# An attention-plus-MLP kernel on one core: x taken transposed out of the values product, head pairs placed on row and column tiles, the MLP spread by hand

## The chip, the cores and the metric

The kernel runs on one core of a Trainium2 chip. The metric is device time in microseconds (us), the median of the runs shown. The core's engines work beside each other: TensorE (PE, and PEld for the loading of its weights), VectorE (DVE), ScalarE (ACT), GpSimd (POOL) and SyncE (SP, here only a queue of DMAs).

## The reference

Eight batches of attention with 12 heads, 448 tokens and 64 values per head, whose softmax has one more term in its denominator, feed an MLP with a squared ReLU.

```python
# q, k, v: (8, 12, 448, 64) f32; w_in: (768, 2048); w_out: (2048, 768)
scores = (1 / sqrt(64)) * q @ k.T                 # 448 x 448 per head
m = max(scores); e = exp(scores - m)
attn = e / (sum(e) + exp(-m) + 1e-9)              # = exp(s) / (sum(exp(s)) + 1)
x = (attn @ v), heads side by side                # 3584 x 768
out = square(maximum(x @ w_in, 0)) @ w_out        # 3584 x 768 f32
```

## The kernel before

`load_batch` (L79) brings one batch of q, k and v in as fp16 with tokens in the partitions: four chunks of 112 tokens, twelve DMAs on POOL's queue (L84 to L86), each moving 112 x 12 runs of 64 values, which are 256 bytes of the f32 source. `load_weights` follows on the same queue (L94, L96). Two batches and the weights are issued before anything else; batch b + 2 is issued after batch b's attention.

`attn_pair` (L98) does two heads. PE transposes the pair's q and k (8 small matmuls, L104 and L109, into the PSUM tile `tp`), DVE copies them to `qkt` (L117 to L119); k lies there twice, once with the upper and once with the lower 64 partitions set to zero by two POOL memsets (L115, L116), so that a product over all 128 partitions gives one head's scores. Per head four matmuls of 448 columns give the scores, keys in the partitions (L130, PSUM `stp`), ACT takes the exponential of two of them at a time (L137, to `et`), and 16 matmuls of 65 columns (L147, PSUM `op`) multiply a 112 x 112 block of `et`, which is loaded as the weights, with the values and a column of ones. So the output has query tokens in its partitions and the sum of exponentials in column 64. DVE adds 1, inverts and multiplies (L157, L164, L165, to `xc`). The MLP needs x with features in the partitions: SP writes `xc` to DRAM (L173) and reads it back with a transposing DMA to `xt` (L177).

The MLP is cut into seven blocks of 512 tokens. `mm1_unit` (L186) does 128 of the 2048 hidden features: six matmuls of 512 columns (L190, PSUM `mp`), then ReLU and squaring on DVE (L198, L204). `mm2_unit` (L207) does 128 tokens by 512 or 256 outputs: 16 matmuls (L213), a scaled copy on ACT (L225), and a DMA out on ACT's queue. One block is 16 + 8 units; after each pair `drain_moe(4)` puts four units into the order of the work, from batch 2 on, block b - 2 being queued with batch b. A scheduler of the framework may reorder instructions of an engine from this program order. The last block comes after all attention.

Of the kernel before, what the change touches and what calls it, by code (L numbers as in the profile page):

```python
# [8 lines left out]
FP32 = mybir.dt.float32  # L10
FP16 = mybir.dt.float16
BF16 = mybir.dt.bfloat16
# [5 lines left out]
def kernel(  # L18
# [14 lines left out]

    P = 112
    NC = S // P
# [3 lines left out]
    TBLK = 512  # L39
    NTB = NT // TBLK  # L40
    NSUB = TBLK // 128

# [6 lines left out]
    qkv_pool = ctx.enter_context(tc.tile_pool(name="qkv", bufs=2))  # L49
    qkt_pool = ctx.enter_context(tc.tile_pool(name="qkt", bufs=4))  # L50
    et_pool = ctx.enter_context(tc.tile_pool(name="et", bufs=4))
    xc_pool = ctx.enter_context(tc.tile_pool(name="xc", bufs=3))
    small = ctx.enter_context(tc.tile_pool(name="small", bufs=8))
    g_pool = ctx.enter_context(tc.tile_pool(name="g", bufs=1))
    r_pool = ctx.enter_context(tc.tile_pool(name="r", bufs=3))
    osb_pool = ctx.enter_context(tc.tile_pool(name="osb", bufs=2))

    st_psum = ctx.enter_context(tc.tile_pool(name="st_psum", bufs=2, space=bass.MemoryType.PSUM))
    o_psum = ctx.enter_context(tc.tile_pool(name="o_psum", bufs=1, space=bass.MemoryType.PSUM))
    tp_psum = ctx.enter_context(tc.tile_pool(name="tp_psum", bufs=1, space=bass.MemoryType.PSUM))  # L60
    moe_psum = ctx.enter_context(tc.tile_pool(name="moe_psum", bufs=2, space=bass.MemoryType.PSUM))

    ident = consts.tile([128, 128], FP16)
    make_identity(nc, ident)

    xt_tiles = [persist.tile([128, NT], FP16, name=f"xt_{c}") for c in range(DCH)]
    win_tiles = [persist.tile([128, DF], FP16, name=f"win_{c}") for c in range(DCH)]
    wout_tiles = [persist.tile([128, DM], FP16, name=f"wout_{c}") for c in range(NFFB)]

    xs_dram = [nc.dram_tensor(f"xstage_{b}", (NPAIR, S, 128), FP16, kind="Internal").ap()  # L70
               for b in range(B)]

    q_r = q.rearrange("b h (c p) d -> b c p h d", p=P)
    k_r = k.rearrange("b h (c p) d -> b c p h d", p=P)
    v_r = v.rearrange("b h (c p) d -> b c p h d", p=P)

    qkv_tiles = {}

    def load_batch(b):  # L79
        qb = qkv_pool.tile([P, NC, H, D], FP16, name="qb")  # L80
        kb = qkv_pool.tile([P, NC, H, D], FP16, name="kb")
        vb = qkv_pool.tile([P, NC, H, D + 1], FP16, name="vb")
        for c in range(NC):
            nc.gpsimd.dma_start(out=qb[:, c, :, :], in_=q_r[b, c])  # L84
            nc.gpsimd.dma_start(out=kb[:, c, :, :], in_=k_r[b, c])  # L85
            nc.gpsimd.dma_start(out=vb[:, c, :, :D], in_=v_r[b, c])  # L86
        nc.gpsimd.memset(vb[:, :, :, D], 1.0)
        qkv_tiles[b] = (qb, kb, vb)

    def load_weights():  # L90
        win_r = moe_w_in.rearrange("(c p) f -> c p f", p=128)
        wout_r = moe_w_out.rearrange("(c p) f -> c p f", p=128)
        for c in range(DCH):
            nc.gpsimd.dma_start(out=win_tiles[c][:, :], in_=win_r[c])  # L94
        for c in range(NFFB):
            nc.gpsimd.dma_start(out=wout_tiles[c][:, :], in_=wout_r[c])  # L96

    def attn_pair(b, pr):  # L98
        hA = 2 * pr
        qb, kb, vb = qkv_tiles[b]  # L100

        qkt_ps = tp_psum.tile([128, 2, S], FP16, name="tp")
        for c in range(NC):
            nc.tensor.transpose(  # L104
                qkt_ps[:, 0, c * P:(c + 1) * P],
                qb[:P, c, hA:hA + 2, :],
# [185 lines left out]
```

## Time and profile before

| What | Value |
|---|---|
| time, median of 2 runs (587.69 and 588.19) | 587.94 us |
| span of the profiled execution | 585.7 us |
| PE busy in the span | 494.6 us (84%) |
| PE weight loads busy | 301.5 us |
| DVE busy | 236.1 us (40%) |
| ACT busy | 197.8 us (34%) |
| POOL busy | 148.7 us (25%) |
| mean granted PE clock | 0.976 |
| HBM read and written | 45.61 MB and 16.52 MB |

The span runs from the first to the last instruction of one profiled execution. That execution has no time of its own in the records, so its span stands beside the median of the runs, which is 2.2 us longer. Busy PE time counts overlapping matmuls once, and the ends of matmuls are modelled. In the rows of groups the columns are: line, engine, operation, tile written and tiles read, shapes, count, then busy time, the mean ns of one, and the engine's idle time just before them with what ended it.

### The profile page before, as it was taken

The page shows a single profiled execution, that of the slowest core. Times are in us where ns is not written, and L with a number is a line of the kernel's source. Part 1 is how long each engine was busy: PE and PEld are TensorE (multiplying, and loading weights), DVE is VectorE, ACT ScalarE, POOL GpSimd, SP SyncE. Part 2 cuts the span into 40 slices and gives each one's busy share as a digit, 9 for nine tenths or more (in the row PEclk, how much of TensorE's full clock was granted, in tenths as well). Part 3 has the DMA queues.
Part 4 walks back from the last instruction along what each step waited for, and adds up shares of the span by engine and source line. Part 5 has one row for each costly group of instructions (what it writes and reads, how often), then busy time and mean ns, then how long its engine had stood idle before and what let it go on. Part 6 is the DMA issues. An engine that isn't in the chain of part 4 may idle for free.

```text
span 585.7 us, 9469 instructions
## 1 busy us (share of the span) xinstructions
PE 494.6 (84%) x3872; PEld 301.5 (51%) x3872; DVE 236.1 (40%) x656; ACT 197.8 (34%) x249; POOL 148.7 (25%) x228
## 2 busy tenths in 40 slices
PE   0100998497999899997999889997999999999997
PEld 0000766364566455564656555564555665566454
DVE  0100555155641276315661157511674237721830
ACT  0000677262433224332434323432325334333011
POOL 9644555531015301071102601134101000000000
PEclk9999999698999899999999989999899999999999
DMA  9999599949119911299113940179111221022002
GB/s 108 128 194 208 96 131 99 123 60 61 32 25 127 148 25 24 60 135 113 25 27 83 162 60 17 32 106 167 25 25 25 71 71 32 20 62 71 21 28 81
DMA packets 183114, 45.44 MB, mean 78 GB/s; under 512 B 176672, under 2 KB 178720, under 8 KB 183072
## 3 DMA queue, kind: packets, MB, share of 16 engines
q0 software_dynamic: 133728, 22.81, 53.3%
q1 hardware_dynamic: 45312, 11.02, 10.5%
q10 hardware_dynamic: 4032, 11.01, 5.1%
q8 instruction: 30, 0.49, 0.3%
q14 instruction: 12, 0.10, 0.1%
HBM read 45.61 MB, written 16.52 MB: 106 GB/s over the span
## 4 chain that ended last, share of the span: by engine, by line
PE 72%; DMA 18%; POOL 4%; issue 2%; DVE 2%; ACT 1%; SPq 0%; POOLq 0%; DVEq 0%
PE mp L190 25%; PE mp L213 20%; PE op L147 14%; PE stp L130 11%; DMA xt<-xstage 6%; DMA xstage<-xc 4%; DMA vb<-in_v_dram 3%; DMA win<-in_moe_w_in_dram 2%; DMA kb<-in_k_dram 1%; POOL vb L86 1%; POOL qb L84 1%; DMA wout<-in_moe_w_out_dram 1%; PE tp L104 1%; PE tp L109 1%; ACT et L137 1%
## 5 line engine op out<-in xcount | busy, mean ns | idle before, releaser
L137 ACT ACTIVATE et<-stp 112x896 f16<-112x896 f32 x192 | 169.1, 915 | 266.8 <-PE stp L130 265.9
L190 PE MATMUL mp<-xt,win 128*128 128x512 f16 x672 | 169.3, 386 | 26.0 <-DMA xt<-xstage 23.0
L213 PE MATMUL mp<-wout,g 128*128 128x512 f16 (+1 forms) x896 | 157.4, 326 | 0.0
L130 PE MATMUL stp<-qkt 128*112 128x448 f16 x384 | 101.5, 373 | 39.1 <-POOL qkt L115 38.3
L147 PEld LDWEIGHTS <-et 112*112 112x112 f16 x1536 | 101.4, 134 | 52.4 <-ACT et L137 27.5
L147 PE MATMUL op<-vb,et 112*112 112x65 f16 x1536 | 109.8, 219 | 4.5 <-DVE xc L165 2.2
L213 PEld LDWEIGHTS <-g 128*128 128x128 f16 x896 | 86.1, 98 | 50.0
L190 PEld LDWEIGHTS <-win 128*128 128x128 f16 x672 | 64.1, 100 | 90.3 <-issue 21.2
L198 DVE TENSOR_SCALAR rt<-mp 128x512 f16<-128x512 f32 x112 | 77.1, 689 | 56.6 <-PE mp L190 52.2
L115 POOL MEMSET qkt<- 64x448 f16 x48 | 22.4, 466 | 229.0 <-PE stp L130 122.4
L117 DVE COPY qkt<-tp 128x448 f16<-128x448 f16 x48 | 18.6, 387 | 137.1 <-PE tp L109 135.8
L130 PEld LDWEIGHTS <-qkt 128*112 128x112 f16 x384 | 41.3, 135 | 59.4 <-POOL qkt L115 38.5
L225 ACT ACTIVATE ot<-mp 128x512 f32<-128x512 f32 (+1 forms) x56 | 27.4, 490 | 116.8 <-PE mp L213 116.8
L157 DVE TENSOR_SCALAR zp<-op 112x4 f32<-112x4 f32 x96 | 15.5, 162 | 124.2 <-PE op L147 124.0
L204 DVE TENSOR_TENSOR g<-rt 128x512 f16<-128x512 f16 x112 | 47.2, 422 | 2.0
L165 DVE TENSOR_TENSOR xc<-op,rcp 112x256 f16<-112x256 f32 x96 | 40.6, 422 | 2.5
L84 POOL DMA_DIRECT2D qb<-in_q_dram x32 | 30.1, 940 | 37.3 <-PE tp L109 35.0
L104 PE MATMUL tp<-ident,qb 112*128 112x112 f16 x192 | 27.8, 220 | 12.6 <-DMA qb<-in_q_dram 11.1
L109 PE MATMUL tp<-ident,kb 112*128 112x112 f16 x192 | 27.5, 219 | 5.0 <-DMA kb<-in_k_dram 5.0
L86 POOL DMA_DIRECT2D vb<-in_v_dram x32 | 29.8, 935 | 7.4 <-PE mp L213 4.9
L85 POOL DMA_DIRECT2D kb<-in_k_dram x32 | 29.9, 935 | 0.0
L104 PEld LDWEIGHTS <-qb 112*128 112x128 f16 x192 | 19.3, 102 | 18.2 <-DMA qb<-in_q_dram 11.6
(15 smaller groups left out, 111.9 us busy)
## 6 DMA issues: line engine op xcount, KB each, us to landing
out_dram<-ot ACTq DMA_DIRECT2D x28, 384.0 KB, 2.6
qb<-in_q_dram POOLq DMA_DIRECT2D x32, 168.0 KB, 5.9
kb<-in_k_dram POOLq DMA_DIRECT2D x32, 168.0 KB, 6.1
vb<-in_v_dram POOLq DMA_DIRECT2D x32, 168.0 KB, 7.2
xstage<-xc SPq DMA_DIRECT2D x48, 112.0 KB, 2.0
win<-in_moe_w_in_dram POOLq DMA_DIRECT2D x6, 512.0 KB, 9.2
wout<-in_moe_w_out_dram POOLq DMA_DIRECT2D x16, 192.0 KB, 7.3
xt<-xstage SPq DMA_TRANSPOSE x48, 2.5
```

The lines of the kernel that those rows point to most:

```text
L84: nc.gpsimd.dma_start(out=qb[:, c, :, :], in_=q_r[b, c])
L86: nc.gpsimd.dma_start(out=vb[:, c, :, :D], in_=v_r[b, c])
L104: nc.tensor.transpose(qkt_ps[:, 0, c * P:(c + 1) * P], qb[:P, c, hA:hA + 2, :], ident[:P, :P],)
L109: nc.tensor.transpose(qkt_ps[:, 1, c * P:(c + 1) * P], kb[:P, c, hA:hA + 2, :], ident[:P, :P],)
L130: nc.tensor.matmul(stp[:P, jj, :S], qkt[:, 1 + hh, jc * P:(jc + 1) * P], qkt[:, 0, :], start=True, stop=True,)
L137: nc.scalar.activation(out=et[:P, 2 * half:2 * half + 2, :], in_=stp[:P, :, :S], func=AF.Exp, scale=scale,)
L147: nc.tensor.matmul(op[:P, ib, :], et[:P, jc, ib * P:(ib + 1) * P], vb[:P, jc, hA + hh, :], start=(jc == 0), stop=(jc == NC - 1),)
L165: nc.vector.tensor_tensor(out=xc[:P, :, h0:h0 + 64], in0=op[:P, :, :D], in1=rcp[:P, :].to_broadcast([P, NC, D]), op=ALU.mult,)
L190: nc.tensor.matmul(hp[:, :TBLK], win_tiles[dc][:, fb * 128:(fb + 1) * 128], xt_tiles[dc][:, t0:t0 + TBLK], start=(dc == 0), stop=(dc == DC ...
L198: nc.vector.tensor_scalar(out=rt[:, :], in0=hp[:, :TBLK], scalar1=0.0, scalar2=GS, op0=ALU.max, op1=ALU.mult,)
L204: nc.vector.tensor_mul(gt[:, :], rt[:, :], rt[:, :])
L213: nc.tensor.matmul(o2[:, :n1 - n0], gtiles[(t, fb)][:, ts * 128:(ts + 1) * 128], wout_tiles[fb][:, n0:n1], start=(fb == 0), stop=(fb == NF ...
```

## The change

- **Tokens.** A batch's 448 tokens lie as 64 partitions x 7 tokens (`RUN`): four of the seven in partitions 0 to 63, three in partitions 64 to 127. A run of a load is then four or three tokens, 1 KB or 768 bytes of the f32 source. Each cut of a batch takes eight DMAs; batch 0 comes in three cuts, the later ones whole, and the weights come in parts between and behind batches 0 and 1. `regroup` has DVE reorder q and k so that a transpose finds two heads side by side.
- **Scores.** No zeroed copies of k and no POOL memsets: head h uses partitions 64h to 64h + 63 of `qkt` as they are, so the two matmuls of a pair of heads address the two row halves of the array. Keys come as three groups of 128 and one of 64; for the last one head h also writes partitions 64h to 64h + 63.
- **Values.** The values are now the weights and `et` is the moving operand, 448 columns at a time. Head h writes partitions 64h to 64h + 63 of `xp`, so the two heads address the two column halves of the array. The output has features in the partitions: it is x transposed. A second set of matmuls with a matrix of 1/256 as weights writes the sum of exponentials to `zp`, repeated over the 64 partitions of each head.
- **Normalising.** ACT takes ln(zp + 1/256) and then exp of its negative; DVE multiplies `xp` by that straight into `xt`. The write to DRAM and the transposing DMA are gone. The factor 256 of the ReLU (L198) moves into this division.
- **MLP.** Blocks of 384 and 512 tokens in turn (3584 in all), the units cut into single matmuls by a generator. The order of the program is kept (`manual_schedule`). One pass of the main loop does the transposes of pair i + 1, half the scores of pair i, MLP work, the other half, the values of pair i - 1, MLP work, and the normalising of pair i - 1. A batch's block is spread over the six passes that follow its last pair, so the first seven passes have no MLP work. The transposes' PSUM tile `tp` now shares the two buffers `mp` of the MLP. Outputs go out on SP's queue, two DMAs for 128 tokens.

```diff
-    P = 112
-    NC = S // P
...
-    TBLK = 512
...
+    RUN = S // 64
+    LO = 4
+    HI = RUN - LO
...
+    nat = ctx.enter_context(tc.tile_pool(name="nat", bufs=2))
+    flat = ctx.enter_context(tc.tile_pool(name="flat", bufs=2))
+    qkt_pool = ctx.enter_context(tc.tile_pool(name="qkt", bufs=3))
+    e_pool = ctx.enter_context(tc.tile_pool(name="e", bufs=2))
+    z_pool = ctx.enter_context(tc.tile_pool(name="z", bufs=2))
+    g_pool = ctx.enter_context(tc.tile_pool(name="g", bufs=2))
+    osb_pool = ctx.enter_context(tc.tile_pool(name="osb", bufs=3))
+    s_psum = ctx.enter_context(tc.tile_pool(name="s_psum", bufs=2, space=bass.MemoryType.PSUM))
+    xz_psum = ctx.enter_context(tc.tile_pool(name="xz_psum", bufs=1, space=bass.MemoryType.PSUM))
+    m_psum = ctx.enter_context(tc.tile_pool(name="m_psum", bufs=2, space=bass.MemoryType.PSUM))
...
+    ctx.enter_context(tc.manual_schedule())
+    nc.scalar.preload_act_table_set("natural_log_exp_and_others")
+    ones = consts.tile([128, 64], FP16)
+    nc.vector.memset(ones, 1.0 / GS)
+    one_b = consts.tile([128, 1], FP32)
+    nc.vector.memset(one_b, 1.0 / GS)
+    xt = persist.tile([128, DCH, NT], FP16, name="xt")
+    win = persist.tile([128, DCH, DF], FP16, name="win")
+    wout = persist.tile([128, NFFB, DM], FP16, name="wout")
+    q_r = q.rearrange("b h (p t) d -> b p h t d", t=RUN)
+    k_r = k.rearrange("b h (p t) d -> b p h t d", t=RUN)
+    v_r = v.rearrange("b (g two) (p t) d -> b two p g t d", two=2, t=RUN)
+    win_r = moe_w_in.rearrange("(c p) f -> p c f", p=128)
+    wout_r = moe_w_out.rearrange("(c p) f -> p c f", p=128)
+    nats, flats = {}, {}
+    def load_batch(b, cuts):
+        qn = nat.tile([128, H, LO, D], FP16, name="qn")
+        kn = nat.tile([128, H, LO, D], FP16, name="kn")
+        vn = nat.tile([128, NPAIR, 2, LO, D], FP16, name="vn")
+        for p0, p1 in cuts:
+            hs = slice(2 * p0, 2 * p1)
+            for t, r in ((qn, q_r), (kn, k_r)):
+                nc.gpsimd.dma_start(out=t[0:64, hs, :, :], in_=r[b, :, hs, 0:LO, :])
+                nc.gpsimd.dma_start(out=t[64:128, hs, 0:HI, :], in_=r[b, :, hs, LO:RUN, :])
+            ps = slice(p0, p1)
+            nc.gpsimd.dma_start(out=vn[0:64, ps, 0, :, :], in_=v_r[b, 0, :, ps, 0:LO, :])
+            nc.gpsimd.dma_start(out=vn[64:128, ps, 0, 0:HI, :], in_=v_r[b, 0, :, ps, LO:RUN, :])
+            nc.gpsimd.dma_start(out=vn[0:64, ps, 1, 1:LO, :], in_=v_r[b, 1, :, ps, 0:HI, :])
+            nc.gpsimd.dma_start(out=vn[64:128, ps, 1, :, :], in_=v_r[b, 1, :, ps, HI:RUN, :])
+        nats[b] = (qn, kn, vn)
+    def load_win(i, n):
+        w = DF // n
+        nc.gpsimd.dma_start(out=win[:, :, i * w:(i + 1) * w], in_=win_r[:, :, i * w:(i + 1) * w])
+    def load_wout(i, n):
+        w = NFFB // n
+        nc.gpsimd.dma_start(out=wout[:, i * w:(i + 1) * w, :], in_=wout_r[:, i * w:(i + 1) * w, :])
+    def regroup(b, p0, p1):
+        hs = slice(2 * p0, 2 * p1)
+        n = 2 * (p1 - p0)
+        both = []
+        for t in nats[b][0:2]:
+            f = flat.tile([128, LO, H // 2, D], FP16, name=f"flat{len(both)}")
+            nc.vector.tensor_copy(f[:, 0:HI, 0:n, :], t[:, hs, 0:HI, :].rearrange("p h t d -> p t h d"))
+            nc.vector.tensor_copy(f[0:64, HI, 0:n, :], t[0:64, hs, HI, :])
+            both.append(f)
+        for pr in range(p0, p1):
+            flats[b, pr] = both, 2 * (pr - p0)
+    def transposes(b, pr):
+        both, h0 = flats.pop((b, pr))
+        hs = slice(h0, h0 + 2)
+        tp = m_psum.tile([128, 2, 512], FP16, name="mp")
+        for i, t in enumerate(both):
+            for s in range(LO):
+                np_ = 128 if s < HI else 64
+                nc.tensor.transpose(tp[:, i, 128 * s:128 * s + np_], t[0:np_, s, hs, :], ident[0:np_, 0:np_])
+        qkt = qkt_pool.tile([128, 2, S], FP16, name="qkt")
+        nc.vector.tensor_copy(qkt, tp[:, :, 0:S])
+        return qkt
+    def scores(qkt, et, ks):
+        for kk in ks:
+            if kk < HI:
+                sp = s_psum.tile([128, 2, 512], FP32, name="sp")
+                for h in range(2):
+                    r = slice(64 * h, 64 * h + 64)
+                    nc.tensor.matmul(sp[:, h, 0:S], qkt[r, 1, 128 * kk:128 * kk + 128], qkt[r, 0, :],
+                                     start=True, stop=True)
+                nc.scalar.activation(out=et[:, 2 * kk:2 * kk + 2, :], in_=sp[:, :, 0:S], func=AF.Exp, scale=scale)
+            else:
+                sp = s_psum.tile([128, 2, 512], FP32, name="sp")
+                for h in range(2):
+                    r = slice(64 * h, 64 * h + 64)
+                    nc.tensor.matmul(sp[r, 0, 0:S], qkt[r, 1, 128 * kk:S], qkt[r, 0, :],
+                                     start=True, stop=True)
+                nc.scalar.activation(out=et[:, 2 * kk, :], in_=sp[:, 0, 0:S], func=AF.Exp, scale=scale)
+    def values(b, pr, et):
+        vn = nats[b][2]
+        xp = xz_psum.tile([128, 512], FP32, name="xp")
+        zp = xz_psum.tile([128, 512], FP32, name="zp")
+        for kk in range(HI):
+            for dst, v in ((xp, True), (zp, False)):
+                for h in range(2):
+                    nc.tensor.matmul(dst[64 * h:64 * h + 64, 0:S],
+                                     vn[:, pr, h, kk + h, :] if v else ones[:, :],
+                                     et[:, 2 * kk + h, :], start=(kk == 0), stop=False)
+        for dst, v in ((xp, True), (zp, False)):
+            for h in range(2):
+                r = slice(64 * h, 64 * h + 64)
+                nc.tensor.matmul(dst[r, 0:S], vn[r, pr, h, HI * (1 - h), :] if v else ones[r, :],
+                                 et[r, 2 * HI, :], start=False, stop=True)
+        lnz = z_pool.tile([128, S], FP32, name="lnz")
+        rcp = z_pool.tile([128, S], FP32, name="rcp")
+        nc.scalar.activation(out=lnz, in_=zp[:, 0:S], func=AF.Ln, bias=one_b)
+        nc.scalar.activation(out=rcp, in_=lnz, func=AF.Exp, scale=-1.0)
+        return xp, rcp
+    def normalise(b, pr, xp, rcp):
+        nc.vector.tensor_mul(xt[:, pr, b * S:(b + 1) * S], xp[:, 0:S], rcp)
+    def mlp(t0, n):
+        gt = []
+        for fb in range(NFFB):
+            hp = m_psum.tile([128, 512], FP32, name="mp")
+            for dc in range(DCH):
+                nc.tensor.matmul(hp[:, 0:n], win[:, dc, fb * 128:(fb + 1) * 128], xt[:, dc, t0:t0 + n],
+                                 start=(dc == 0), stop=(dc == DCH - 1))
+                if dc < DCH - 1:
+                    yield n / 2.4
+            rt = r_pool.tile([128, 512], FP16, name="rt")
+            nc.vector.tensor_scalar(out=rt[:, 0:n], in0=hp[:, 0:n], scalar1=0.0, scalar2=None, op0=ALU.max)
+            g = g_pool.tile([128, 512], FP16, name=f"g{fb}")
+            nc.vector.tensor_mul(g[:, 0:n], rt[:, 0:n], rt[:, 0:n])
+            gt.append(g)
+            yield n / 2.4
+        for ts in range(n // 128):
+            ot = osb_pool.tile([128, DM], FP32, name="ot")
+            for n0, n1 in ((0, 512), (512, DM)):
+                op = m_psum.tile([128, 512], FP32, name="mp")
+                for fb in range(NFFB):
+                    nc.tensor.matmul(op[:, 0:n1 - n0], gt[fb][:, ts * 128:(ts + 1) * 128], wout[:, fb, n0:n1],
+                                     start=(fb == 0), stop=(fb == NFFB - 1))
+                    if fb < NFFB - 1:
+                        yield (n1 - n0) / 2.4
+                nc.scalar.activation(out=ot[:, n0:n1], in_=op[:, 0:n1 - n0], func=AF.Copy, scale=OUT_SCALE)
+                if n1 < DM:
+                    yield (n1 - n0) / 2.4
             for half in range(2):
+                seg = (t0 + ts * 128) // 64 + half
+                b, j = seg // RUN, seg % RUN
+                t = j // 2 + LO * (j % 2)
+                rows = out[b * S:(b + 1) * S, :].rearrange("(p t) m -> t p m", t=RUN)
+                nc.sync.dma_start(out=rows[t], in_=ot[64 * half:64 * half + 64, :])
+            yield (DM - 512) / 2.4
+    load_batch(0, ((0, 1), (1, 3), (3, 6)))
+    for i in range(4):
+        load_win(i, 8)
+    load_batch(1, ((0, 3), (3, 6)))
+    for i in range(4, 8):
+        load_win(i, 8)
+    for i in range(4):
+        load_wout(i, 4)
+    blocks = []
+    t0 = 0
+        n = 384 if b % 2 == 0 else 512
+        blocks.append((t0, n))
+        t0 += n
+    work = []
+    def drain(ns):
+        while work and ns > 0:
+            got = next(work[0], None)
+            if got is None:
+                work.pop(0)
+            else:
+                ns -= got
+    def block_ns(n):
+        return (NFFB * DCH * n + (n // 128) * NFFB * DM) / 2.4
+    pairs = [(b, pr) for b in range(B) for pr in range(NPAIR)]
+    NP = len(pairs)
+    qkts, ets = {}, {}
+    regroup(0, 0, 1)
+    regroup(0, 1, 3)
+    qkts[0] = transposes(*pairs[0])
+    share = 0.0
+    for i in range(NP + 1):
+        if i < NP:
+            b, pr = pairs[i]
+            if pr == 0 and 0 < b and b + 1 < B:
+                load_batch(b + 1, ((0, 6),))
+            if pr == 1:
+                regroup(b, 3, 6)
+            if pr == 4 and b + 1 < B:
+                regroup(b + 1, 0, 3)
+            if i + 1 < NP:
+                qkts[i + 1] = transposes(*pairs[i + 1])
+            et = ets[i] = e_pool.tile([128, RUN, S], FP16, name="et")
+            scores(qkts[i], et, (0, 1))
+            drain(share * 0.5)
+            scores(qkts[i], et, (2, 3))
+            qkts.pop(i)
+        if i > 0:
+            done = values(*pairs[i - 1], ets.pop(i - 1))
+        drain(share * 0.5)
+        if i > 0:
+            normalise(*pairs[i - 1], *done)
+            pb, ppr = pairs[i - 1]
+            if ppr == NPAIR - 1:
+                work.append(mlp(*blocks[pb]))
+                share = block_ns(blocks[pb][1]) / NPAIR
+    drain(1e12)
```

More of the change, by code (lines that the diff above doesn't have):

```diff
@@ L5 @@
 import concourse.tile as tile
-from concourse import bass_utils, mybir
+from concourse import mybir
 from concourse.masks import make_identity
@@ L68 @@
[L68 to L88, printed above, removed]
```

171 lines of the change are left out of this document (removed).

## The prediction

> **What bounds the kernel now.** I read the page first: busy shares, the slices, the shares of the chain.
>
> ```profile
> span 585.7 us, 9469 instructions
> ...
> PE 494.6 (84%) x3872; PEld 301.5 (51%) x3872; DVE 236.1 (40%) x656; ACT 197.8 (34%) x249; POOL 148.7 (25%) x228
> ...
> PE   0100998497999899997999889997999999999997
> ...
> PE 72%; DMA 18%; POOL 4%; issue 2%; DVE 2%; ACT 1%; SPq 0%; POOLq 0%; DVEq 0%
> ```
>
> PE carries 72% of the chain and is busy 84% of the span. The slices say where it isn't: the first four (14.6 us each) are nearly empty, after that PE runs at 8 or 9 tenths with one hole near slice 8. So there are three parts: a start, a body set by PE, and a tail. The timeline shows what the start is.
>
> ```profile
> 1.35 1.05 POOL L84 DMA_DIRECT2D qb<-in_q_dram  x1 [0.40 <-issue]
> ...
> 5.53 0.27 PE L104 MATMUL tp<-ident,qb 112*128 112x112 f16 x1 [5.53 <-DMA qb<-in_q_dram]
> ...
> 57.64 0.53 POOL L96 DMA_DIRECT2D wout<-in_moe_w_out_dram  x1 [0.38 <-DMA wout<-in_moe_w_out_dram]
> 58.21 0.47 POOL L115 MEMSET qkt<- 64x448 f16 x1
> ...
> 58.73 1.74 PE L130 MATMUL stp<-qkt 128*112 128x448 f16 x4 [38.31 <-POOL qkt L115]
> ```
>
> The first transposes run at 5.5 us, but the first scores wait until 58.73 us for a POOL memset (L115), which stands on POOL behind the issues of two batches and all weights. That is 58.7 us in which PE does almost nothing.
>
> For the body I look at PE's timeline over one period deep in the run, then at PE's groups with shapes kept apart, and at one long stretch (its columns: length, busy time of PE, PEld, DVE, ACT, POOL, the granted clock, DMA share and GB/s).
>
> ```profile
> 292.12 1.00 PE L147 MATMUL op<-vb,et 112*112 112x65 f16 x16
> 292.95 1.68 PE L190 MATMUL mp<-xt,win 128*128 128x512 f16 x7
> 294.46 0.21 PE L104 MATMUL tp<-ident,qb 112*128 112x112 f16 x1
> ...
> 294.81 0.21 PE L109 MATMUL tp<-ident,kb 112*128 112x112 f16 x1
> 294.86 1.68 PE L190 MATMUL mp<-xt,win 128*128 128x512 f16 x7
> 296.52 0.94 PE L130 MATMUL stp<-qkt 128*112 128x448 f16 x4
> ...
> 303.64 0.21 PE L104 MATMUL tp<-ident,qb 112*128 112x112 f16 x1
> ```
>
> ```profile
> L190 PE MATMUL mp<-xt,win 128*128 128x512 f16 x672 | 169.3, 386 | 26.0 <-DMA xt<-xstage 23.0 <-DMA kb<-in_k_dram 3.0
> L213 PE MATMUL mp<-wout,g 128*128 128x512 f16 x448 | 110.2, 379 | 0.0
> ...
> L130 PE MATMUL stp<-qkt 128*112 128x448 f16 x384 | 101.5, 373 | 39.1 <-POOL qkt L115 38.3 <-ACT et L137 0.6 <-DVE qkt L118 0.2
> ```
>
> ```profile
> 101.00:470.00 369.00, 341.31 (x2662) 207.53 (x2661) 162.41 (x454) 136.20 (x171) 89.15 (x135) 0.96 0.65 70
> ```
>
> From the first transpose of one pair at 294.46 to that of the next at 303.64 is a period of 9.18 us: one pair and four MLP units. The units' price is read in the tail, where nothing else runs:
>
> ```profile
> 540.21 20.72 PE mp L190 x96
> 560.93 20.81 PE mp L213 x128
> ```
>
> 96 matmuls of 512 columns take 20.72 us, 216 ns each (the 379 to 386 ns of a single one is latency, which overlaps); 128 of both widths take 20.81 us. A block of 512 tokens is thus 41.53 us, and seven are 290.7 us. Four units of the first kind take 24 x 0.216 = 5.18 us, which leaves 4.00 us of the period to the attention of a pair. Of that the eight transposes are about 0.40 (starts 0.05 us apart), the eight score matmuls 8 x 0.189 = 1.51 (four took 0.94 us, the last of them 0.373 from start to end, so three steps are 0.57), and the rest, 2.09 us, is the 32 short matmuls of the values.
>
> The parts add up: start 58.7, MLP 290.7, attention 48 x 4.00 = 192, waits of L190 for DMAs 26.0 (that group's idle time, nearly all for `xt`), end 585.7 - (560.93 + 20.81) = 4.0, and the clock of 0.96 in the body, 0.04 x 369 = 15. Sum 586, span 585.7.
>
> **The change, part by part.** The sum is made against the span; the median of the runs is 2.2 us above it.
>
> *Start.* POOL's memsets go, and pair 0 comes first. One POOL issue of 128 runs is 0.53 us (the `wout` row); the first cut's eight issues end at 1.35 + 8 x 0.54 = 5.7, the second's at 10. What they move is limited by the rate at the start of before, where the slices of 1.55 us show 155 GB/s for q, k, v and 207 for weights:
>
> ```profile
> GB/s 0 0 98 85 146 153 156 155 156 155 156 156 132 12 112 112 148 155 155 156 155 189 205 211 198 198 211 214 217 217 214 193 207 207 205 207 206 206 207 210
> ```
>
> Two cuts are half a batch, 1.0 MB, and at 155 GB/s take 6.6 us from about 3 us on, so the issues decide. A first load took 4.2 us from issue to use. DVE reorders both cuts before it copies pair 0's transposes (the program order), so the first scores come at about 10 + 3 + 2.5 = 15.5 us. Ends: 12 (no order on DVE) and 22 (all of batch 0).
>
> *Seven passes without MLP work.* ACT sets them.
>
> ```profile
> L137 ACT ACTIVATE et<-stp 112x896 f16<-112x896 f32 x192 | 169.1, 915 | 266.8 <-PE stp L130 265.9 <-ACT et L137 0.3
> L225 ACT ACTIVATE ot<-mp 128x512 f32<-128x512 f32 x28 | 16.7, 597 | 81.0 <-PE mp L213 81.0
> L225 ACT ACTIVATE ot<-mp 128x256 f32<-128x256 f32 x28 | 10.7, 383 | 35.8 <-PE mp L213 35.8
> ```
>
> From the two L225 rows 256 columns cost 383 ns and 512 cost 597, so a column is 0.84 ns and 448 columns take about 0.54 us. Three exponentials of 896 at 0.915, one of 448, the logarithm and the second exponential: 2.75 + 3 x 0.54 = 4.37 us. PE's part is less (below), so 7 x 4.37 = 30.6; the first MLP matmul comes at 46 us. Nothing of the weights is late: half of `win` and batch 1 follow batch 0, and the whole of before's early loads ended by 60 us at lower or equal rates; `wout` is needed at about 46 + 3 x 8 = 70. Batch 2's loads stand behind it on POOL and are 12 us of transfer, wanted at about the same time: up to 5 us once, kept for the range.
>
> *MLP in the body.* Blocks 0 to 6 are four of 384 and three of 512 tokens. Columns stay the same: 384 tokens are 0.75 x 41.53 = 31.2, together 4 x 31.2 + 3 x 41.53 = 249.3 us; block 7, the tail, 41.5.
>
> *Attention of a pair on PE.* Transposes: 896 columns as before, 0.40 us. Scores: eight matmuls, values: sixteen, all 448 columns, that is 24, or twelve twos. This trace has no two matmuls in different parts of the array, so a two costs between 0.189 (side by side) and 0.378 us (one after the other, the pitch of L130). I take 0.189: the two read different partitions or write different ones, and no tile of the one is named by the other, so of the known rows the single matmul is the nearest. 12 x 0.189 = 2.27, with the transposes 2.67 us instead of 4.00.
>
> [...]
>
> *Change of tile shape.* A pass goes from whole-array matmuls to the last q transpose (64 partitions), back, to the last k transpose, MLP, scores, 64 x 64 scores, values, 64 x 64 values, MLP: nine changes. A change costs between nothing (L147 to L190 to L104 follow each other with no gap, though their shapes differ) and a whole latency less its pitch, 379 - 216 = 163 ns. I take 0.05 us, nearer to the rows without a gap: 0.45 us a pass.
>
> *Other small gaps of a pass.* A period of before has none that is left over; I allow 0.17 us, for `tp` now waits for a buffer of `mp`. The low end is nothing, since a pass can't be shorter than its matmuls; the high end is the first rival.
>
> Body: 249.3 + 42 x (2.67 + 0.45 + 0.17) = 249.3 + 138.2 = 387.5 us.
>
> *DMA round trip.* `xt` is written by DVE, so the 26 us go. I take the clock's 15 us to go with these holes; if they stay, 494, within the range. What is late next: nothing by DMA, since a batch is issued one batch ahead, some 40 us, and 12 us long. The outputs move from ACT's queue to SP's, empty now.
>
> *DVE.*
>
> ```profile
> L198 DVE TENSOR_SCALAR rt<-mp 128x512 f16<-128x512 f32 x112 | 77.1, 689 | 56.6 <-PE mp L190 52.2
> L204 DVE TENSOR_TENSOR g<-rt 128x512 f16<-128x512 f16 x112 | 47.2, 422 | 2.0
> L165 DVE TENSOR_TENSOR xc<-op,rcp 112x256 f16<-112x256 f32 x96 | 40.6, 422 | 2.5
> ...
> L117 DVE COPY qkt<-tp 128x448 f16<-128x448 f16 x48 | 18.6, 387 | 137.1 <-PE tp L109 135.8 <-POOL qkt L116 0.6
> ```
>
> Per pass with 512 tokens in the first half of a block: 5.33 units x (0.689 + 0.422) = 5.9; the copy of 896 columns, twice L117 at most, 0.77; the normalising of 448 f32 columns, between L165's 256 (422 ns) and L198's 512 (689), 0.62; and in one such pass per batch a `regroup`, four copies of 1152 and 384 elements, at L117's and L204's 0.55 ns per element and 0.14 fixed, 2.3 us. Sum 9.6 us against PE's 6.92 + 3.29 = 10.2. It hides, but by little; without that cover PE waits for `mp`.
>
> Sum: 46 + 387.5 + 41.5 + 4.0 = 479 us of span, 481 us of time.
>
> **The rivals.**
>
> *DVE or the two `mp` buffers bind.* For: the 9.6 against 10.2, and `tp` takes one of the two buffers while another holds a half-done unit. Against: in the second half of a block DVE has almost nothing. If each of the 112 units of blocks 0 to 6 waits 0.3 us, 34 us: 515 us.
>
> *Each change of shape empties the array.* At the upper bound, 163 ns, nine changes are 1.47 us a pass, 1.02 more than I took: 42 x 1.02 = 43, so 524 us. Against: no gap at the changes of shape in the trace, but all of those start at partition 0 of what they read and write. [...]
>
> *The twos do not overlap* (the change doesn't do what it says). A two is 0.378: 42 x 2.27 = 95 more, and the seven early passes become PE's at 5.0, 5 more: 581 us, no change from before, for the start and the round trip pay for it.
>
> *Slower: the twos do not even follow each other closely*, each small matmul ends before one on another tile begins. Then 24 x 0.373 = 8.95 us a pass instead of 2.27: 42 x 6.68 = 281, and 35 in the early passes: about 797 us. It decides from the point where a two costs 0.189 + (600 - 481) / (42 x 12) = 0.425 us, a little above the serial price. For it: only that latency and pitch differ so much (373 and 189 ns). Against: L147 and L104 show PE overlapping matmuls of different weights.
>
> **How the numbers follow.** A measurement here tells 2% from no change: 576 and 600 us are the marks. Chances: forecast (460 to 500 us) 0.50; better than 460, with free changes of shape and an earlier start, 0.05; DVE or buffers 0.14; drains 0.15; no overlap 0.10; slower 0.06. The predicted time is the forecast's, 481. The range goes from 450 (changes free, start at 12 us, no small gaps: 481 - 19 - 3.5 - 7) to 560 (drains and buffers together, 558) and leaves out the last two and little else. Faster by over 2%: the first four, 0.84; within 2%: no overlap, 0.10; slower 0.06.
>
> **What would show it.** First scores near 15 us, first MLP matmul near 46. The two matmuls of a two starting within some 20 ns of each other, twos 0.19 us apart; if 0.38, no overlap. Gaps on PE at the nine places of a pass: under 0.1 us, or about 0.16 with drains. PE waiting for `rt` or `qkt` on DVE in the first half of a block: the buffer rival. No wait for `xt` by a DMA, and a clock of 1.00 in the body. I am wrong if passes with 512-token blocks last over 11 us, or with 384 over 9.3 (my sums: 10.2 and 8.5).

## The result, and the profile after

The changed kernel takes 508.16 us (median of 2 runs, 505.82 and 510.51) beside 587.94: a ratio of 0.8646, with a 95% interval of 0.855 to 0.874. The profiled execution took 510.51 us, its span is 508.7. The forecast was 481 with a range of 450 to 560. Of the kernel with short runs, further down, one execution took 1193.8 us and the other three 506.9 to 510.9, so that one is left out of its ratio, and its profile, which is of that one, gives no pass lengths.

The page of the changed kernel, the same lines as before (its span, the busy times, PE in 40 slices, the chain by engine):

```profile
span 508.7 us, 7575 instructions
...
PE 479.7 (94%) x3200; PEld 235.3 (46%) x3200; DVE 214.8 (42%) x422; ACT 231.5 (46%) x345; POOL 68.9 (14%) x106
...
PE   1877899999999999999999999999999999999996
...
PE 90%; ACT 4%; DVE 2%; POOL 1%; DMA 1%; issue 0%; DVEq 0%; POOLq 0%
```

PE is now 94% busy and 90% of the chain. Of the four nearly empty slices at the start one is left, and the four behind it are at 7 and 8 tenths. Three stretches of the same execution follow (columns: length, busy time of PE, PEld, DVE, ACT, POOL, granted clock, DMA share, GB/s): up to the first MLP matmul, the 42 passes with MLP work, the tail.

```profile
0.00:54.86 54.86, 35.98 (x228) 14.77 (x229) 13.53 (x31) 28.74 (x41) 38.76 (x63) 0.91 1.22 161
54.86:462.65 407.79, 402.18 (x2751) 198.77 (x2750) 183.45 (x359) 198.50 (x296) 30.10 (x43) 1.00 0.36 58
462.65:508.70 46.05, 41.52 (x224) 21.71 (x222) 17.86 (x32) 4.30 (x9) 0.00 (x0) 0.98 0.17 44
```

```profile
462.65 20.72 PE mp L175 x96
483.37 20.82 PE mp L190 x128
```

Beside the sum of the prediction: first scores at 13.2 us (15.5 were forecast), first MLP matmul at 54.86 (46), body 407.8 (387.5), tail 20.72 + 20.82 = 41.5 (41.5), end 508.7 - 504.2 = 4.5 (4.0). The 30 us over the forecast are 8.9 up to the first MLP matmul (11.1 more in the early passes, 2.3 less ahead of them), 20.3 in the body and 0.5 at the end. The first scores, from the timeline of the start:

```profile
13.20 0.93 PE L134 MATMUL sp<-qkt 64*128 64x448 f16 x4
```

The early passes are from there to 54.86: 41.7 us for seven, 5.9 each where 4.37 were forecast. PE's timeline of one of them, and ACT's groups:

```profile
24.36 0.93 PE L134 MATMUL sp<-qkt 64*128 64x448 f16 x4
25.98 0.37 PE L134 MATMUL sp<-qkt 64*128 64x448 f16 x2 [0.68 <-ACT et L136]
26.78 0.38 PE L141 MATMUL sp<-qkt 64*64 64x448 f16 x2 [0.44 <-ACT et L136]
...
29.53 0.57 PE L134 MATMUL sp<-qkt 64*128 64x448 f16 x4
```

```profile
L136 ACT ACTIVATE et<-sp 128x896 f16<-128x896 f32 x144 | 126.0, 915 | 155.0 <-PE sp L134 154.6
L162 ACT ACTIVATE lnz<-zp,one_b 128x448 f32<-128x448 f32 x48 | 30.4, 633 | 41.9 <-PE zp L158 41.9
L163 ACT ACTIVATE rcp<-lnz 128x448 f32<-128x448 f32 x48 | 27.7, 576 | 1.5
L143 ACT ACTIVATE et<-sp 128x448 f16<-128x448 f32 x48 | 26.0, 542 | 0.0
```

ACT's own work in a pass is 3 x 0.915 + 0.542 + 0.633 + 0.576 = 4.50 us, close to the forecast. But from 24.36 to 29.53 are 5.17 us, and PE stands idle for 0.68 and 0.44 us before the second half of the scores: these stand ahead of the values in program order and wait for ACT's first exponentials. When PE then does the values, ACT waits for it. The clock adds to it, 0.91 up to the first MLP matmul: a two (two matmuls on two halves of the array) takes 0.37 us instead of 0.19 in some of these passes. The granted clock doesn't tell all of it: it reads 1.00 up to 30 us, yet the twos that start at 20.43 and 20.80 us are 0.37 apart as well.

PE's timeline of one pass of the body (a block of 384 tokens; the count behind x is of matmuls, two to a two):

```profile
302.63 0.57 PE L134 MATMUL sp<-qkt 64*128 64x448 f16 x4
303.14 2.77 PE L175 MATMUL mp<-xt,win 128*128 128x384 f16 x16
305.85 0.36 PE L134 MATMUL sp<-qkt 64*128 64x448 f16 x2
306.14 0.38 PE L141 MATMUL sp<-qkt 64*64 64x448 f16 x2
306.44 0.38 PE L152 MATMUL xp<-et,vn 128*64 128x448 f16 x2
306.66 0.36 PE L152 MATMUL zp<-et,ones 128*64 128x448 f16 x2
306.85 0.36 PE L152 MATMUL xp<-et,vn 128*64 128x448 f16 x2
...
307.42 0.35 PE L152 MATMUL zp<-et,ones 128*64 128x448 f16 x2
307.70 0.38 PE L158 MATMUL xp<-et,vn 64*64 64x448 f16 x2
307.91 0.35 PE L158 MATMUL zp<-et,ones 64*64 64x448 f16 x2
308.20 2.77 PE L175 MATMUL mp<-xt,win 128*128 128x384 f16 x16
...
311.64 0.57 PE L134 MATMUL sp<-qkt 64*128 64x448 f16 x4
```

From 302.63 to 311.64 are 9.01 us; 8.49 were forecast. Twos follow each other 0.19 us apart (306.66, 306.85). Where the shape of the tiles changes, 0.28 to 0.30 pass instead: 305.85 to 306.14 (64 x 128 to 64 x 64), 306.14 to 306.44 (to 128 x 64), 307.42 to 307.70 (to 64 x 64), 307.91 to 308.20 (to the whole array). By the start times of the single instructions, a change costs 95 ns at most of its places, 104 and 118 ns at the two around the 64 x 64 scores, and in the transposes 151 and 132 ns pass where 56 and about 30 are due. The nine of a pass sum to 0.90 us.

What passes in that tenth isn't shown. The weights' loads (PEld) beside the values are one hint:

```profile
315.52 0.11 PEld L152 LDWEIGHTS <-vn 128*64 128x64 f16 x2 [0.20 <-issue]
315.52 0.38 PE L152 MATMUL xp<-et,vn 128*64 128x448 f16 x2
315.54 0.11 PEld L152 LDWEIGHTS <-ones 128*64 128x64 f16 x2
315.73 0.35 PE L152 MATMUL zp<-et,ones 128*64 128x448 f16 x2
```

Within a shape the weights of the next two (`ones`) start to load 0.19 us ahead of their matmuls (315.54 and 315.73). Behind a change they start only with their matmuls (both at 315.52), and a load takes 0.11 us, about what a change costs. So whether the array empties first, as the rival had it, or only a load that did not run ahead is paid, these traces don't tell apart.

What is left of PE's waits in the body is small:

```profile
PE mp L123 <- DVE rt L180: 2.3, 7, 0.4
PE mp L175 <- DVE qkt L125: 1.9, 1, 1.9
PE mp L123 <- ACT ot L194: 1.4, 3, 0.5
```

### The profile page after: what moved, and what is told of

Read it like the earlier page. It is cut to its first block, busy times and chain, and to the rows that moved or that the text cites. A ratio compares the mean times of both kernels' runs of the same rounds, so it can differ in the third digit from the quotient of the medians.

```text
span 508.7 us, 7575 instructions
## 1 busy us (share of the span) xinstructions
PE 479.7 (94%) x3200; PEld 235.3 (46%) x3200; DVE 214.8 (42%) x422; ACT 231.5 (46%) x345; POOL 68.9 (14%) x106
## 4 chain that ended last, share of the span: by engine, by line
PE 90%; ACT 4%; DVE 2%; POOL 1%; DMA 1%; issue 0%; DVEq 0%; POOLq 0%
PE mp L190 29%; PE mp L175 28%; PE xp L152 7%; PE mp L123 6%; PE zp L152 6%; PE sp L134 6%; PE sp L141 3%; PE xp L158 3%; ACT et L136 2%; PE zp L158 2%; DVE rt L180 1%; DMA kn<-in_k_dram 1%; ACT lnz L162 1%; ACT rcp L163 1%; ACT ot L194 0%
## 5 line engine op out<-in xcount | busy, mean ns | idle before, releaser
L136 ACT ACTIVATE et<-sp 128x896 f16<-128x896 f32 x144 | 126.0, 915 | 155.0 <-PE sp L134 154.6
L175 PE MATMUL mp<-xt,win 128*128 128x384 f16 (+1 forms) x768 | 153.2, 353 | 1.9 <-DVE qkt L125 1.9
L190 PE MATMUL mp<-wout,g 128*128 128x512 f16 (+1 forms) x896 | 152.9, 326 | 0.0
L190 PEld LDWEIGHTS <-g 128*128 128x128 f16 x896 | 84.3, 98 | 67.6 <-issue 14.9
L180 DVE TENSOR_SCALAR rt<-mp 128x384 f16<-128x384 f32 (+1 forms) x128 | 79.9, 624 | 77.1 <-PE mp L175 69.3
L167 DVE TENSOR_TENSOR xt<-xp,rcp 128x448 f16<-128x448 f32 x48 | 29.8, 621 | 147.4 <-ACT rcp L163 147.4
L123 PE MATMUL mp<-ident,flat 128*128 128x128 f16 (+1 forms) x384 | 43.6, 222 | 14.3 <-DVE flat L109 10.5
L152 PE MATMUL xp<-et,vn 128*64 128x448 f16 x288 | 55.0, 378 | 0.0
L152 PE MATMUL zp<-et,ones 128*64 128x448 f16 x288 | 54.0, 372 | 0.0
L182 DVE TENSOR_TENSOR g<-rt 128x384 f16<-128x384 f16 (+1 forms) x128 | 50.1, 391 | 4.4
L134 PE MATMUL sp<-qkt 64*128 64x448 f16 x288 | 46.4, 366 | 5.6 <-ACT et L136 5.6
L162 ACT ACTIVATE lnz<-zp,one_b 128x448 f32<-128x448 f32 x48 | 30.4, 633 | 41.9 <-PE zp L158 41.9
## 6 DMA issues: line engine op xcount, KB each, us to landing
kn<-in_k_dram POOLq DMA_DIRECT2D x6, 384.0 KB, 10.2
```

Of the source, the lines that this page charges most:

```text
L123: nc.tensor.transpose(tp[:, i, 128 * s:128 * s + np_], t[0:np_, s, hs, :], ident[0:np_, 0:np_])
L134: nc.tensor.matmul(sp[:, h, 0:S], qkt[r, 1, 128 * kk:128 * kk + 128], qkt[r, 0, :], start=True, stop=True)
L136: nc.scalar.activation(out=et[:, 2 * kk:2 * kk + 2, :], in_=sp[:, :, 0:S], func=AF.Exp, scale=scale)
L152: nc.tensor.matmul(dst[64 * h:64 * h + 64, 0:S], vn[:, pr, h, kk + h, :] if v else ones[:, :], et[:, 2 * kk + h, :], start=(kk == 0), stop ...
L162: nc.scalar.activation(out=lnz, in_=zp[:, 0:S], func=AF.Ln, bias=one_b)
L167: nc.vector.tensor_mul(xt[:, pr, b * S:(b + 1) * S], xp[:, 0:S], rcp)
```

## The experiments

Ten kernels ran. The ratios are to the kernel before, which ran beside them on the same chip, and times are medians of four executions unless said otherwise; single passes are read from each run's trace (in the changed kernel three of the six passes of a 384-token block take 8.85 us, from transposes to transposes, and these are the ones compared). Theory A says that a change of tile shape costs PE about 0.10 us and that this is what the body lost; theory C says that the early passes are a chain through PE and ACT.

### The changed kernel again

> The changed kernel once more, as the yardstick of the runs beside it: 504 to 511 us, with passes of about 9.0 us for blocks of 384 tokens in the body and a first MLP matmul near 55 us.

507.7 us, ratio 0.8646 (0.859 to 0.871). In this profile the first MLP matmul comes at 50.0 us instead of 54.9, because the clock was halved less in the early passes (the granted clock reads 1.00 over the first 55 us, where the profile above has 0.91); the passes of the body are the same to 0.01 us. So about 5 us of the early stretch vary from run to run. At full speed the early passes settle at 5.07 us here (the first scores of two of them start at 39.31 and 44.38 us).

### Two changes of shape fewer, two more

```diff
-        for i, t in enumerate(both):
-            for s in range(LO):
+        for s in range(LO):            # grouped: seven changes a pass
+            for i, t in enumerate(both):
```

> The transposes of a pass are put in another order: the three whole-height ones of q and of k first, then the two of 64 partitions, so that a pass changes tile shape seven times instead of nine; nothing else moves. Theory A (each change of tile shape costs PE about 0.10 us, which the trace of the changed kernel shows as starts of 282 ns where 186 are due): 0.2 us less a pass, 8 us less over the 42 passes with MLP work and about 1 in the seven early ones, 499 us beside 508. Rival B (the lost time sits in the transposes because their weights come late or because their tile waits for a buffer of the MLP, and not in the number of changes): no difference, within 2 us.

501.9 us, ratio 0.854 (0.849 to 0.860). The 8.85 us passes became 8.64.

```diff
-            for s in range(LO):
+            for s in (0, 3, 1, 2):     # spread: eleven changes a pass
```

> The opposite: the 64-partition transpose is put second of four, for q and for k, so that a pass changes tile shape eleven times instead of nine. Theory A: 0.2 us more a pass, 8 to 9 us more in all, 517 us beside 508. Rival B: no difference, within 2 us.

519.1 us, ratio 0.883 (0.876 to 0.890). The 8.85 us passes became 9.06.

Seven, nine and eleven changes give passes of 8.64, 8.85 and 9.06 us: 0.105 us for each, in both directions, with the same instructions in all three. Theory A holds and rival B falls. The whole times moved by 6 and 11 us; 42 x 0.21 = 8.8 were due, and the rest is within what the early passes vary.

### What the column tiles' overlap is worth

```diff
-        for kk in range(HI):
-            for dst, v in ((xp, True), (zp, False)):
-                for h in range(2):
+        for h in range(2):
+            for kk in range(HI):
+                for dst, v in ((xp, True), (zp, False)):
```

> In the values product the six whole-height matmuls of one head are issued first, then the six of the other (the 64-row ones stay as they were), so that no two that follow each other lie on different column tiles. The number of changes of tile shape stays. If the two heads run side by side now (starts 3 ns apart, 189 ns for both), six twos become twelve single matmuls: 6 x 0.186 = 1.12 us more a pass, 47 us in the 42 passes and up to 8 in the early ones, 555 to 565 us. If the overlap is only in how the profile models ends and starts, and the array takes turns anyway: no difference from 508.

529.4 us, ratio 0.902 (0.896 to 0.907): neither. A pass took 9.26 us, 0.41 more instead of 1.12. PE's timeline of the values in this kernel:

```profile
307.69 0.38 PE L152 MATMUL xp<-et,vn 128*64 128x448 f16 x1
307.90 0.35 PE L152 MATMUL zp<-et,ones 128*64 128x448 f16 x1
308.09 0.38 PE L152 MATMUL xp<-et,vn 128*64 128x448 f16 x2
308.28 0.38 PE L152 MATMUL zp<-et,ones 128*64 128x448 f16 x2
308.47 0.38 PE L152 MATMUL xp<-et,vn 128*64 128x448 f16 x2
308.66 0.38 PE L152 MATMUL zp<-et,ones 128*64 128x448 f16 x2
308.88 0.35 PE L152 MATMUL xp<-et,vn 128*64 128x448 f16 x1
309.07 0.35 PE L152 MATMUL zp<-et,ones 128*64 128x448 f16 x1
```

In program order six matmuls of one head (xp, zp, xp, zp, xp, zp) come before six of the other. The first two start alone; then four times two start together, xp with xp and zp with zp, and two end alone. That fits only if the first matmul of the second head starts with the third of the first, ahead of three that stand before it in program order. Twelve matmuls thus took eight places instead of six, and 2 x 0.19 = 0.38 us is the 0.41 measured. The order in the program was not enough to keep the tiles apart, so the next kernel puts both heads on the same column half.

```diff
-                    nc.tensor.matmul(dst[64 * h:64 * h + 64, 0:S],
+                    nc.tensor.matmul(dst[0:64, 0:S],
...
-                                     et[:, 2 * kk + h, :], start=(kk == 0), stop=False)
+                                     et[:, 2 * kk + h, :], start=(kk == 0 and h == 0), stop=False)
...
-                                 et[r, 2 * HI, :], start=False, stop=True)
+                                 et[r, 2 * HI, :], start=(h == 1), stop=True)
```

> The changed kernel, but the whole-height matmuls of the values product write partitions 0 to 63 for both heads, so no two of them lie on different column tiles in any order (head 1's sums over the first 384 keys are added to head 0's instead of its own: this part of the computation is changed). Theory: the column tiles overlap fully in the changed kernel, and putting the heads in turn cost only 0.41 us a pass because PE started matmuls of the second head before those of the first, with up to four of these between; here it can't, and six twos become twelve singles: 6 x 0.186 = 1.12 us more a pass, 555 to 565 us. Rival: what the heads in turn showed, 0.41 us a pass, is all that the overlap is worth: 525 to 533 us.

561.6 us, ratio 0.957 (0.951 to 0.963). A pass took 9.98 us, 1.13 more; 1.12 were due.

```profile
317.37 0.57 PE L152 MATMUL xp<-et,vn 128*64 128x448 f16 x2
317.77 0.54 PE L152 MATMUL zp<-et,ones 128*64 128x448 f16 x2
318.15 0.54 PE L152 MATMUL xp<-et,vn 128*64 128x448 f16 x2
```

Two matmuls of a row, which were followed by the next two after 0.19 us, are now followed after 0.38 to 0.40. So the overlap of the column tiles is complete, and in the values alone it is worth 54 us of this kernel.

### The values early in the passes without MLP work

```diff
             scores(qkts[i], et, (0, 1))
+            early = i > 0 and not work
+            if early:
+                done = values(*pairs[i - 1], ets.pop(i - 1))
             drain(share * 0.5)
             scores(qkts[i], et, (2, 3))
...
-        if i > 0:
+        if i > 0 and i - 1 in ets:
             done = values(*pairs[i - 1], ets.pop(i - 1))
```

> Only the seven passes without MLP work are changed: the values product of the pair before is put ahead of the second half of the scores, so that PE has work while ACT takes the first two exponentials. Theory C (these passes last 5.1 to 7.2 us because PE, in program order, waits for ACT and ACT then for PE, and the idle PE has its clock halved now and then; ACT's own work is 0.633 + 0.576 + 0.542 + 3 x 0.915 = 4.50 us): they become ACT's, about 4.6 us each, so the first MLP matmul comes 3 to 8 us earlier and the time is 500 to 505 us beside 508. Rival D (late loads set these passes): no difference, within 2 us.

501.2 us, ratio 0.853 (0.847 to 0.859). The early passes settle at 4.69 us, and PE's only wait in them is for ACT:

```profile
28.85 0.80 PE L134 MATMUL sp<-qkt 64*128 64x448 f16 x4 [0.72 <-ACT et L136]
...
33.54 0.80 PE L134 MATMUL sp<-qkt 64*128 64x448 f16 x4 [0.72 <-ACT et L136]
```

From 28.85 to 33.54 are 4.69 us, ACT's 4.50 and a little. The first MLP matmul came at 48.3 us. Theory C holds; the loads did not set these passes, so rival D falls. The clock read 1.00 all through this run. Beside the 5.07 us that the same passes settle at in the changed kernel's repeat, also at full speed, the new order is worth 0.38 us a pass; the spans of these two traces, 503.8 and 500.5 us, differ by 3.3. The medians differ by 6.5, so about half of the gain came with the order at the same clock; the rest fits the clock, but no run shows that part by itself.

### The start alone, in the kernel before

```diff
-        nc.gpsimd.memset(qkt[64:, 1, :], 0.0)
-        nc.gpsimd.memset(qkt[:64, 2, :], 0.0)
+        nc.vector.memset(qkt[64:, 1, :], 0.0)
+        nc.vector.memset(qkt[:64, 2, :], 0.0)
```

> The kernel before with one thing changed: its two memsets per pair go from POOL's queue to DVE, so that they no longer stand behind the issues of the loads. Theory: the first scores come near 20 us instead of 58.7; the weights still end at about 60 us, and the twelve pairs of batches 0 and 1 that need none fill the time until then, so some 38 us go: 545 to 555 us. Rival (the early time was hidden by the loads of the weights anyway, and the MLP starts no earlier): 580 us or more.

567.4 us, ratio 0.963 (0.955 to 0.971): between the two. The chain that ended last in this kernel, in order of time (start, length, what):

```profile
18.87 1.74 PE stp L130 x4
31.12 13.16 DMA xstage<-xc
46.18 11.71 DMA xstage<-xc
59.08 10.46 DMA xstage<-xc
```

The first scores came at 18.87 us instead of 58.73, 40 us earlier, and half of that was lost again: the DMA that writes `xc` to DRAM took 13, 12 and 10 us while the weights' loads filled the DMA engines (nine tenths busy or more in each of the page's first seven slices, to 99.6 us; the median of that DMA in the kernel before is 2.0 us), and with three `xc` buffers the attention stood still. PE's wait for `xc` (total, times, longest), and the stretch from 60 to 100 us (columns as above):

```profile
PE op L147 <- DVE xc L165: 14.8, 4, 8.4
60.00:100.00 40.00, 23.12 (x161) 16.88 (x161) 9.70 (x38) 13.79 (x16) 18.68 (x22) 0.54 1.68 144
```

In the kernel before that wait is 2.2 us in all, and the clock in the same stretch 1.00. What a halved clock makes of the values is in the trace of the kernel before: sixteen of their matmuls take 1.66 us at 110.63 us, where it is 0.50, and 0.97 at 120.06, where it is 1.00. The first MLP matmul then came at 99.85 us, 10 earlier than the 109.80 of the kernel before. So taking the memsets off POOL is worth 20 us as long as the round trip is there; the other 20 went to waits for `xc` and to a slower clock, in shares that this run doesn't separate. That they need the round trip gone fits this chain; a kernel with that alone was not run.

### Six changes a pass, and the early values

```diff
+        between()                      # in values: ahead of the 64-row matmuls
         for dst, v in ((xp, True), (zp, False)):
...
-            scores(qkts[i], et, (2, 3))
+                scores(qkts[i], et, (2,))
+                last = lambda q=qkts[i], e=et: scores(q, e, (3,))
...
+                    done = values(*pairs[i - 1], ets.pop(i - 1), last)
```

(with the grouped transposes and the early values as above)

> Three things together in the changed kernel: transposes grouped by height, the 64 x 64 scores put between the whole-height and the 64-row values so that they share one stretch of 64 x 64 tiles (six changes of tile shape a pass instead of nine), and the values early in the passes without MLP work. If a change costs 0.10 us wherever it stands: 0.31 us less a pass, 13 us, and with the 3 to 8 us of the early passes 486 to 493 us. If only the transposes' changes cost: 497 us or more.

489.1 us, ratio 0.833 (0.827 to 0.838), the fastest of all. Passes of 8.85 us became 8.52: three changes fewer, 0.33 us. In its timeline the 64 x 64 scores and values follow each other without the extra tenth:

```profile
307.17 0.36 PE L152 MATMUL zp<-et,ones 128*64 128x448 f16 x2
307.45 0.38 PE L141 MATMUL sp<-qkt 64*64 64x448 f16 x2
307.67 0.35 PE L159 MATMUL xp<-et,vn 64*64 64x448 f16 x2
```

From 307.17 to 307.45 is a change (0.28 us); from the 64 x 64 scores at 307.45 to the 64 x 64 values at 307.67 are 0.22, where the changed kernel has 0.30.

### Short runs, no regrouping

```diff
+        shape = [128, H, LO, D] if b < 2 else [128, LO, H, D]
...
+                if b >= 2:
+                    for s in range(RUN):
+                        p = slice(64 * (s // LO), 64 * (s // LO) + 64)
+                        nc.gpsimd.dma_start(out=t[p, s % LO, :, :], in_=r[b, :, :, s, :])
+                    continue
...
+        if b >= 2:                     # in regroup: nothing is copied
+            for pr in range(p0, p1):
+                flats[b, pr] = nats[b][0:2], 2 * pr
+            return
```

> Batches 2 to 7 of the changed kernel load q and k token by token, in runs of 256 bytes, straight into the order that the transposes want, so DVE regroups nothing for them; batches 0 and 1 stay as they were. Theory: in the body loads are hidden whatever their runs, and the four regrouping copies, 2.1 us of DVE each time, are what makes the first and the fifth pass of each batch longer than their neighbours (9.34 beside 8.91, 11.21 beside 10.79): 0.5 to 1 us less a batch, 503 to 505 us beside 508. Rival (the short runs come late or disturb): equal or above 508, with PE waiting for a DMA of q or k.

506.9 to 510.9 us, ratio 0.868 (0.861 to 0.875).

> The same put on top of the three things of the kernel with six changes a pass. Theory: 3 to 5 us below its 489, so 484 to 486 us. Rival: equal or above 489.

489.8 us, ratio 0.836 (0.831 to 0.842), beside 489.1. DVE was busy 192.7 us instead of 213.7, and the passes are the same to 0.01 us, the longer ones too (9.01, the first of a 384-token block, and 10.88, the fifth of a 512-token block). So the theory falls: the regrouping was hidden, and the longer passes are not its doing. What they hold instead are the waits quoted above, 0.32 to 0.35 us at the end of each block's first pass and 0.47 at the end of the fifth of 512 tokens, where the transposes wait for a buffer of `mp` that DVE's ReLU or ACT's output copy has not yet freed. For batches 2 to 7 the 1 KB runs and the regrouping together are worth nothing that these runs show; for batches 0 and 1 it wasn't tried.

## Why the prediction was right, and where it missed

The direction and the range were right, and the likeliest time was 27 us too low.

**Start.** Right: 13.2 us instead of 15.5, set by POOL's issues and DVE's regrouping in program order. The early loads of the kernel before ran on past the 60 us that I read, to about 64, but nothing came of it: PE has no wait for weights in the changed kernel.

**Seven passes without MLP work: the step "ACT sets them" failed.** ACT's work was sized about right (4.50 against 4.37), but the order of the program makes PE and ACT take turns, and the sum took PE's clock for full there without a reason. The seven passes took 41.7 us, 11.1 more than forecast. As an estimate from the repeat's 5.07 us a pass, 0.9 of that is ACT's work, 4.0 the turns, and the remaining 6.2 the halved clock. With the values moved ahead ACT does set them, at 4.69 us.

**Twos at 0.189 us.** Right, and shown by the kernel that takes the overlap away: two of 448 columns on two column halves follow the two before after 0.19 us, as single ones do with the heads in turn (307.90, 308.09), and after 0.38 on one half.

**Change of tile shape: the term was mis-sized, 0.05 us for 0.10.** Nine a pass make 0.90 instead of 0.45, over 42 passes 19 of the body's 20.3 us. The traces show that each change costs time; that the array empties at one they don't show. The price is between the two ends I gave, nothing and 163 ns. The row without a gap that I leaned on (L147 to L190) was no evidence: going between 112 and 128 rows or columns cost nothing (L190 starts 0.05 us after the L147 ahead of it, as one L147 does after another), going to a half cost 95 ns or more. The measured time lies between the forecast and the rival in which the array empties (524), which took the upper bound.

**DVE and the `mp` buffers.** The rival is there, but small: 2.3 + 1.9 + 1.4 = 5.6 us of waits in all, 0.13 us a pass, against the 0.17 I allowed. The normalising took 0.62 us as estimated, the copy of `tp` 0.62 (0.77 at most).

**Round trip and clock.** Right: no wait for `xt`, and a clock of 1.00 in the body. The 26 us were sized by where the waits stood in the kernel before. In the run with the early start L190's waits for `xt` are about the same, 27.0 us, but waits for `xc` of 14.8 us (2.2 before) come beside them, so the round trip costs more once the start no longer hides it.

**The signs set in advance.** Passes over 9.3 us with 384 tokens or over 11 with 512 were to mean that I was wrong. Averaged over a block they took 8.97 and 10.77, but single ones went over: 9.34, and 11.07 and 11.21. The changes of shape at twice their price are the larger part of what the averages hold beyond my 8.5 and 10.2.

**Where the 77 us came from.** By the same parts: the start 58.7 to 13.2, 45.5 us; the waits for `xt` and the slower clock, 41 (its 15 for the clock being the prediction's estimate); the end -0.5; the MLP nothing. Attention was 48 x 4.00 = 192 and is now 41.7 + (407.8 - 249.3) = 200, so -8; together 78. In the body a pair costs 3.77 us instead of 4.00; the matmuls saved 1.33, as forecast, and the changes of shape and small gaps took 1.1 of it back. So by these sums the packed attention gained 9.5 us in the body and lost 18 in the early passes, and with its values on one column half it would be 54 us longer still: the packing paid for the new layout, it did not make the kernel faster. The order of the start and the missing round trip did. Of the first, the run with the early start alone is the evidence, for 20 of its 45 us; the second is read from the waits in the trace of before, and a kernel without the round trip alone was not run.

## What to carry to other kernels

In this kernel two matmuls on two halves of the array cost what one costs, 0.19 us, and each change of tile shape cost about 0.1 us: count the changes through the whole pass (a short transpose counts too), and group the work by shape; in this kernel that was a matter of order alone and gave some 12 us (489 beside 501, both with the values early). Where an engine's total suggests that it sets a stage, follow the program order once through the stage: two engines that wait for each other in turn take longer than either (5.07 us a pass here, where ACT alone has 4.50). And a wait that is removed shows its worth only when what hid behind it is gone as well: an earlier start alone gave half back, to DMAs that now ran beside the loads and to a slower clock behind them.

## What the runs showed of the hardware that was not expected

PE did not keep matmuls of different column tiles in program order: with the heads in turn, a matmul of the second tile started with the third of the first, ahead of three others. The evidence is the starts in this trace (one each at 307.69 and 307.90 us, two at 308.09) and the pass that grew by 0.41 us instead of 1.12. The run with grouped transposes has a second sign, on row halves: a score matmul starts at 304.49 us and the last transpose, which stands ahead of it in program order, at 304.52. That fits head 1's, since the transposes of 64 partitions read partitions 0 to 63 and head 1's scores the others. That PE did this, and not the framework, rests on the kernel's order of the program being kept (`manual_schedule`); no run shows the stream of instructions itself.

By the starts in the pass shown, the price of a change of tile shape was nearly the same in every direction that it has, 95 to 118 ns, between whole-array, 64-row, 64-column and 64 x 64 tiles. Score matmuls of 64 x 128 right behind transposes of 64 x 128 cost none: in the pass shown they start at 302.63 us, 0.01 us after the last transpose.
